# Decoding one of two weight matrices in natural order and exchanging its columns later, with a new instruction plan

## The chip, the cores and the metric

The kernel runs on 1 core of one Trainium2 chip. The metric is the device time of one execution in microseconds (us), as the median of several runs. In texts and rows below, PE is TensorE, which does the matrix products (PEld its loads of weights), DVE is VectorE, ACT is ScalarE, POOL is GpSimd and SP is SyncE, whose queue issues the transfers (DMAs).

## What is computed

Attention with pooled keys and values over 8 batches, 8 heads, 576 positions and 64 columns, and then a layer of 4608 tokens whose activation is a rational function. Cut to what matters:

```
k_p, v_p = k, v averaged over groups of 8 positions        # 72 keys per head
attn = softmax(q @ k_p^T / sqrt(64));  x = attn @ v_p       # x: 4608 x 512
h = x @ w_in                                               # w_in: 512 x 2048
P = a0 + a1 h + a2 h^2 + a3 h^3
Q = 1 + |b0| |h| + |b1| h^2
out = (P / (Q + 1e-6)) @ w_out                             # w_out: 2048 x 512
```

The two weight matrices arrive as 64-bit floating-point numbers, two 32-bit words each, and the kernel makes 32-bit numbers of them itself (the decoding).

## The kernel before

**Tiling.** The 4608 tokens are 18 blocks (i) of 256, the 2048 hidden columns 8 slices (u) of 256. A step is a pair (i, u). `mm1` multiplies x of the block by slice u of w_in into a bank of PSUM `ph`. It makes 24 products of 256 columns, since x and the weights are each split into a high part and a low part (`x0`, `x1`; `w[:, 0]`, `w[:, 1]`) and three of the four pairings are kept. `rational` and `quotient` turn `ph` into the activation on ACT, DVE and POOL, with the tiles `t`, `w`, `r`, `rp` (a PSUM bank) and the results `gh` (high, ACT) and `gl` (low, POOL). `mm2` multiplies these by slice u of w_out, 12 products of 512 columns, into two PSUM banks `po`, which collect over the slices. `po` leaves through `ob` to memory. All PSUM tiles share 8 banks.

**Attention** (`prep_k`, `prep_v`, `attention`, `values`) is computed block by block between these steps: q is transposed (`qT`, from block 4 on by DVE, before that by PE as `pq`), the scores go to `ps`, DVE takes maximum and difference into `e`, ACT the exponential, the transposed probabilities are `am`, and the product with the values is `pv`, which becomes `x0`, `x1`.

**Decoding** (`load_weights`, line 489) is done once for each of the 16 slices (8 of w_in, 8 of w_out), one at a time when a slice is first needed, in the first 200 us. A load of 1 MiB brings 128 x 1024 pairs of words (`rwin`, `rwout`). Then five instructions follow, each on 128 x 1024 elements: ACT scales the high words (Prelu) into `m`; DVE shifts `m`; DVE joins it with the low words (`scalar_tensor_tensor`); ACT copies `m` to the high part, rounding it; POOL subtracts this from `m` for the low part. The pool `dec` of the tile `m` has two buffers. For w_in, ACT and DVE read every second word (8 bytes apart) and write next to each other. For w_out, the columns change places as they are decoded: even and odd columns come to lie in two halves, as `mm2` reads them. So they read every fourth word (16 bytes apart), one half after the other, and copy and subtraction work on neighbouring elements:

```
words = raw.bitcast(I32).rearrange("p (n b t) -> p t b n", b=2, t=2)
hw, lw = words[:, 1], words[:, 0]
whole, bits = (y.rearrange("p (b n) -> p b n", b=2) for y in (m, mi))
```

**Order.** Every instruction is recorded by the class `Plan` with an engine, an assumed length and a due time, and `solve` puts them in an order: of what can start next on an engine, that with the earliest due time goes first. `issue` writes them out, so that all go through one line, L307 in the trace. The assumed lengths come from `Engine` (a fixed part and a rate per element); an argument such as `W + 260` lengthens one. Due times come from `due` (constants `HEAD`, `PACE`, `SLOW`, line 939), go back along the dependences, and are moved by the table `LATER` (line 114), which gives for an instruction's number the us by which it is due later. Where the plan has PE idle, `issue` puts in products that change nothing (fillers, L299): at first onto the tile `idle`, later with a zero operand onto an open `po`.

Of the kernel before, what the change touches and what calls it, by code (L numbers as in the profile page):

```python
# [8 lines left out]
F32 = mybir.dt.float32  # L9
F32R = mybir.dt.float32r  # L10
I32 = mybir.dt.int32
# [88 lines left out]
class Plan:  # L100
# [13 lines left out]
    LATER = {  # L114
# [12 lines left out]
    }  # L127
# [198 lines left out]
def tile_pooled_attention_then_rational_moe(  # L326
# [162 lines left out]
    def load_weights(kind, u):  # L489
        name = f"{kind}{u}"  # L490
        raw = new("cpool", name, [P, 2 * CW], F32, "r" + name)
        if kind == "win":
            dma(1024, raw.bitcast(I32).rearrange("p (k x) -> p k x", x=4 * P),
                w_in32[:, u * 4 * P:(u + 1) * 4 * P].rearrange("(k p) x -> p k x", p=P))
        else:
            dma(1024, raw.bitcast(I32).rearrange("p (f x) -> p f x", f=2),
                w_out32[u * 2 * P:(u + 1) * 2 * P, :].rearrange("(f p) x -> p f x", p=P), run=4096)
        m = new("dec", "m", [P, CW], F32, f"m_{name}")
        mi = m.bitcast(I32)
        if kind == "win":  # L500
            words = raw.bitcast(I32).rearrange("p (n t) -> p t n", t=2)
            hw, lw = words[:, 1], words[:, 0]
            whole, bits = m, mi
        else:

            words = raw.bitcast(I32).rearrange("p (n b t) -> p t b n", b=2, t=2)
            hw, lw = words[:, 1], words[:, 0]
            whole, bits = (y.rearrange("p (b n) -> p b n", b=2) for y in (m, mi))
        act(CW + 100).activation(whole, hw.bitcast(F32), AF.Prelu, scale=2.0 ** -111, alpha=-2.0 ** 32)
        dve(CW, port=True, rate=0.52).tensor_scalar(  # L510
            out=mi, in0=mi, scalar1=3, scalar2=None, op0=ALU.logical_shift_left)
        dve(CW, port=True).scalar_tensor_tensor(
            out=bits, in0=lw, scalar=29, in1=bits, op0=ALU.logical_shift_right,
            op1=ALU.bitwise_or)
        w = new("cpool", name, [P, 2, CW], F32R, name)
        act(CW).copy(w[:, 0, :], m)
        gp(CW).tensor_tensor(out=w[:, 1, :], in0=m, in1=w[:, 0, :].bitcast(F32),
                             op=ALU.subtract)
        weights[kind, u] = w
# [108 lines left out]
    def split_v(n, vs, vrs, port):  # L628
        vhi, vlo = vm[n % 2]
        for hh, msk in enumerate((mlo, mhi)):  # L630
            cols = slice(hh * D, (hh + 1) * D)
            act(NJ * D + 100).activation(vhi[:, :, cols], vs, AF.Copy, scale=msk)
            dve(NJ * D, port=port).scalar_tensor_tensor(
                out=vlo[:, :, cols], in0=vs, scalar=msk,
                in1=vhi[:, :, cols].bitcast(F32), op0=ALU.mult, op1=ALU.subtract)
        r = vr[n % 2].rearrange("p (c m) x -> p c m x", m=2)
        for m in range(2):
            dst = r[:, :, m, :]
            act(2 * D + 100).activation(dst, vrs, AF.Copy, scale=mrem_lo[m])
            dve(2 * D, port=port).scalar_tensor_tensor(  # L640
                out=dst, in0=vrs, scalar=mrem[m], in1=dst.bitcast(F32),
# [31 lines left out]
    def attention(t, hi, lo, qs, es):  # L673
# [34 lines left out]
        for c in range(2):  # L708
# [9 lines left out]
        ef = es[:, 0:NJ, t % 2]  # L718
        act(H * SP).activation(ef, ef, AF.Exp, scale=D ** -0.5)
        dve(H * SP).tensor_reduce(out=sm.rearrange("p (j h) -> p j h", h=2), in_=e, op=ALU.add,  # L720
                                  axis=AX.X)
        dve(0).tensor_scalar(out=sm, in0=sm, scalar1=1e-9, scalar2=None, op0=ALU.add)
        dve(40).reciprocal(sm, sm)
# [135 lines left out]
    def quotient(W, h, t, w, r, rp, gh, gl, early, late):  # L859
# [14 lines left out]
            out=t, in0=rp, scalar=-2.0, in1=t, op0=ALU.add, op1=ALU.mult)  # L874
        act(W, claims=late).copy(gh, t)
        gp(W).tensor_tensor(out=gl, in0=t, in1=gh.bitcast(F32), op=ALU.subtract)
# [61 lines left out]
    order += [(i, u) for i in range(4, NBLK) for u in range(NU)]  # L938
    HEAD, PACE, SLOW, SLOWS = 15.0, 5.4, 5.0, 2 * NA

# [80 lines left out]
```

## Time and profile before

| | us |
|---|---|
| median of 3 runs | 941.05 (940.32 to 942.04) |
| the profiled execution | 940.58 |
| its span, first to last instruction | 938.9 |
| PE busy | 897.4 (96%) |
| DVE busy | 775.9 (83%) |
| ACT busy | 697.5 (74%) |
| POOL busy | 529.1 (56%) |
| mean granted clock of PE | 0.994 of full speed |

The profiled execution lasted 1.7 us longer than its span and is 0.05% below the median. Busy time of PE contains the fillers and the time by which single products are late, so that it is read with the pace of the products beside it. Most transfers of inputs and weights are in the first 80 us, where the 16 DMA engines are near fully busy; later they are a third busy or less.

### The profile page before, as it was taken

The page shows a single profiled execution, that of the slowest core. Times are in us where ns is not written, and L with a number is a line of the kernel's source. Part 1 is how long each engine was busy: PE and PEld are TensorE (multiplying, and loading weights), DVE is VectorE, ACT ScalarE, POOL GpSimd, SP SyncE. Part 2 cuts the span into 40 slices and gives each one's busy share as a digit, 9 for nine tenths or more (in the row PEclk, how much of TensorE's full clock was granted, in tenths as well). Part 3 has the DMA queues.
Part 4 walks back from the last instruction along what each step waited for, and adds up shares of the span by engine and source line. Part 5 has one row for each costly group of instructions (what it writes and reads, how often), then busy time and mean ns, then how long its engine had stood idle before and what let it go on. Part 6 is the DMA issues. An engine that isn't in the chain of part 4 may idle for free.

```text
span 938.9 us, 17065 instructions
## 1 busy us (share of the span) xinstructions
PE 897.4 (96%) x6157; PEld 830.8 (88%) x6157; DVE 775.9 (83%) x1337; ACT 697.5 (74%) x1124; POOL 529.1 (56%) x472
## 2 busy tenths in 40 slices
PE   8888998899999999999999999999989999999997
PEld 7877987898898999898998889998989999999996
DVE  7799987788988888887989699969797888787674
ACT  4888887777766776867786767686857787777774
POOL 4776775667355645454754474456544654445443
PEclk9999999999999999999999999999999999999999
DMA  9993210146143503030522252123413321202000
GB/s 310 309 386 115 62 36 1 45 123 146 48 90 77 122 6 73 9 65 22 126 61 43 49 121 71 27 53 90 103 25 62 89 58 20 61 1 57 1 24 23
DMA packets 185081, 75.33 MB, mean 80 GB/s; under 512 B 162340, under 2 KB 162340, under 8 KB 184996
## 3 DMA queue, kind: packets, MB, share of 16 engines
q1 hardware_dynamic: 184996, 74.23, 31.1%
q8 instruction: 49, 0.80, 0.3%
q14 instruction: 36, 0.29, 0.1%
HBM read 50.59 MB, written 12.58 MB: 67 GB/s over the span
## 4 chain that ended last, share of the span: by engine, by line
DVE 28%; PE 28%; ACT 16%; issue 9%; POOL 9%; SPq 6%; DMA 3%; DVEq 0%; POOLq 0%; ACTq 0%
PE ph L307 13%; PE po L307 12%; DVE t L307 12%; SPq L307 6%; POOL w L307 5%; ACT rp L307 4%; DVE rp L307 3%; POOL gl L307 3%; DVE m_wout L307 2%; ACT gh L307 2%; DVE e L307 2%; PE ps L307 2%; ACT w L307 2%; ACT r L307 2%; ACT t L307 2%
## 5 line engine op out<-in xcount | busy, mean ns | idle before, releaser
L307 PEld LDWEIGHTS ph<-x,win 128*128 128x128 f32 x3264 | 461.6, 192 | 41.0 <-ACT x L307 3.5
L307 PE MATMUL ph<-x,win 128*128 128x256 f32 x3264 | 473.1, 277 | 6.9 <-ACT x L307 2.5
L307 PE MATMUL po<-wout,gh 128*128 128x512 f32 x1152 | 335.9, 386 | 10.5 <-ACT gh L307 8.1
L307 POOL TENSOR_TENSOR w<-w,r 128x512 f32<-128x512 f32 (+1 forms) x145 | 192.3, 1327 | 260.5 <-ACT r L307 252.2
L307 POOL TENSOR_TENSOR gl<-t,gh 128x512 fp32r<-128x512 f32 (+1 forms) x145 | 189.5, 1307 | 96.3 <-ACT gh L307 86.6
L307 PEld LDWEIGHTS po<-wout,gh 128*128 128x128 f32 x1152 | 186.9, 192 | 22.9 <-ACT gh L307 10.9
L307 PE MATMUL po<-wout,gl 128*128 128x512 f32 x576 | 171.8, 383 | 0.8 <-POOL gl L307 0.8
L307 DVE SCALAR_TENSOR_TENSOR t<-t,abn,rp 128x512 f32<-128x512 f32 (+1 forms) x145 | 107.0, 738 | 69.4 <-ACT rp L307 68.4
L307 ACT ACTIVATE rp<-w,cbias 128x512 f32<-128x512 f32 (+1 forms) x145 | 99.7, 688 | 53.6 <-POOL w L307 48.9
L307 ACT ACTIVATE w<-ph 128x512 f32<-128x512 f32 (+1 forms) x145 | 85.6, 591 | 60.8 <-DVE t L307 35.4
L307 DVE TENSOR_TENSOR t<-t,ph 128x512 f32<-128x512 f32 (+1 forms) x145 | 97.8, 674 | 38.3 <-ACT t L307 32.9
L307 ACT ACTIVATE t<-ph,abn 128x512 f32<-128x512 f32 (+1 forms) x145 | 111.6, 770 | 17.4 <-PE ph L307 10.4
L307 ACT ACTIVATE r<-w,abn 128x512 f32<-128x512 f32 (+1 forms) x145 | 117.4, 810 | 8.9 <-POOL gl L307 2.8
L307 ACT CAST gh<-t 128x512 fp32r<-128x512 f32 (+1 forms) x145 | 89.0, 614 | 40.7 <-DVE t L307 40.1
L307 DVE SCALAR_TENSOR_TENSOR t<-t,abn,ph 128x512 f32<-128x512 f32 (+1 forms) x145 | 106.5, 735 | 7.3 <-ACT w L307 3.8
L307 DVE SCALAR_TENSOR_TENSOR t<-rp,t 128x512 f32<-128x512 f32 (+1 forms) x145 | 98.4, 679 | 1.8
L307 DVE SCALAR_TENSOR_TENSOR rp<-w,rp 128x512 f32<-128x512 f32 (+1 forms) x145 | 98.9, 682 | 0.9 <-ACT rp L307 0.5
L307 PEld LDWEIGHTS po<-wout,gl 128*128 128x128 f32 x576 | 92.2, 191 | 5.6 <-POOL gl L307 2.0
L307 ACT ACTIVATE rp<-rp 128x512 f32<-128x512 f32 (+1 forms) x145 | 84.0, 579 | 2.9 <-DVE t L307 0.5
L307 POOL TENSOR_TENSOR e<-e,sm 128x576 f32<-128x576 f32 x36 | 41.6, 1170 | 29.3 <-DVE sm L307 23.0
L307 PE MATMUL ps<-kpT,qT 128*128 128x144 f32 (+1 forms) x304 | 45.4, 299 | 8.8 <-DVE qT L307 5.9
L307 PEld LDWEIGHTS ps<-kpT,qT 128*128 128x128 f32 (+1 forms) x304 | 37.3, 181 | 15.8 <-DVE qT L307 7.4
(109 smaller groups left out, 883.2 us busy)
## 6 DMA issues: line engine op xcount, KB each, us to landing
am<-e SPq DMA_DIRECT2D x224, 48.0 KB, 2.1
out_dram<-ob SPq DMA_DIRECT2D x17, 512.0 KB, 3.5
rwin<-in_moe_w_in_dram SPq DMA_DIRECT2D x8, 1024.0 KB, 12.2
rwout<-in_moe_w_out_dram SPq DMA_DIRECT2D x8, 1024.0 KB, 14.6
st_k<-in_k_dram SPq DMA_DIRECT2D x12, 512.0 KB, 4.6
st_v<-in_v_dram SPq DMA_DIRECT2D x12, 512.0 KB, 3.8
q<-in_q_dram SPq DMA_DIRECT2D x144, 32.0 KB, 2.0
st_v<-in_v_dram SPq DMA_DIRECT2D x48, 64.0 KB, 2.2
```

Of the source, the lines that this page charges most:

```text
L307: getattr(engines[op.eng], name)(*map(value, args), **{k: value(v) for k, v in kw.items()})
```

## The change

`load_weights` no longer treats w_out apart up to the joined `m`: ACT and DVE read every second word, and `m` is in natural order. The columns change places in the last two instructions: the copy (ACT) and the subtraction (POOL) read `m` at every second element (8 bytes apart) and write the two halves. `mm2` is as it was. The plan gets other assumed lengths (Prelu of the decoding, the low parts of the values, exp, the copy to `gh`), one small DVE instruction of the softmax is planned as one that needs the port which DVE and POOL share, steps are due 5.5 and then 5.8 us apart in place of 5.0 and 5.4, and `LATER` has other numbers (they reach to instruction 4701; before, to 1655).

```diff
     LATER = {
-        40: -21840.4, 45: -7931.8, 50: -6005.5, 61: -3867.9, 77: -7203.6, 85: -2.3, 99: -5839.5,
...
+        1: -25, 40: -21825, 45: -7954, 50: -6055, 61: -3895, 77: -7198, 85: 11, 99: -5792, 127: 63,
...
-        if kind == "win":
-            words = raw.bitcast(I32).rearrange("p (n t) -> p t n", t=2)
-            hw, lw = words[:, 1], words[:, 0]
-            whole, bits = m, mi
-        else:
-
-            words = raw.bitcast(I32).rearrange("p (n b t) -> p t b n", b=2, t=2)
-            hw, lw = words[:, 1], words[:, 0]
-            whole, bits = (y.rearrange("p (b n) -> p b n", b=2) for y in (m, mi))
-        act(CW + 100).activation(whole, hw.bitcast(F32), AF.Prelu, scale=2.0 ** -111, alpha=-2.0 ** 32)
+        words = raw.bitcast(I32).rearrange("p (n t) -> p t n", t=2)
+        hw, lw = words[:, 1], words[:, 0]
+        act(CW + 200).activation(m, hw.bitcast(F32), AF.Prelu, scale=2.0 ** -111, alpha=-2.0 ** 32)
...
         dve(CW, port=True).scalar_tensor_tensor(
-            out=bits, in0=lw, scalar=29, in1=bits, op0=ALU.logical_shift_right,
+            out=mi, in0=lw, scalar=29, in1=mi, op0=ALU.logical_shift_right,
             op1=ALU.bitwise_or)
         w = new("cpool", name, [P, 2, CW], F32R, name)
-        act(CW).copy(w[:, 0, :], m)
-        gp(CW).tensor_tensor(out=w[:, 1, :], in0=m, in1=w[:, 0, :].bitcast(F32),
-                             op=ALU.subtract)
+        high, low = w[:, 0, :], w[:, 1, :]
+        if kind == "wout":
+
+            m, high, low = (m.rearrange("p (n b) -> p b n", b=2),
+                            *(x.rearrange("p (b n) -> p b n", b=2) for x in (high, low)))
+        act(CW).copy(high, m)
+        gp(CW).tensor_tensor(out=low, in0=m, in1=high.bitcast(F32), op=ALU.subtract)
...
-            dve(NJ * D, port=port).scalar_tensor_tensor(
+            dve(NJ * D + 50, port=port).scalar_tensor_tensor(
...
-        act(H * SP).activation(ef, ef, AF.Exp, scale=D ** -0.5)
+        act(H * SP + 36).activation(ef, ef, AF.Exp, scale=D ** -0.5)
...
-        dve(0).tensor_scalar(out=sm, in0=sm, scalar1=1e-9, scalar2=None, op0=ALU.add)
+        dve(0, port=True).tensor_scalar(out=sm, in0=sm, scalar1=1e-9, scalar2=None, op0=ALU.add)
...
-        act(W, claims=late).copy(gh, t)
+        act(W + 26, claims=late).copy(gh, t)
...
-    HEAD, PACE, SLOW, SLOWS = 15.0, 5.4, 5.0, 2 * NA
+    HEAD, PACE, SLOW, SLOWS = 15.0, 5.8, 5.5, 2 * NA
```

No engine's instructions change in kind or number but for the fillers: 52 onto `idle` and 29 onto `po` before, 54 and 6 with the change. What stands in another order is seen at three places.

On DVE, while w_out's slices 5 and 6 are decoded (`m_wout5`, `m_wout6`; `t2_5`, `rp2_5` belong to the activation of block 2, slice 5; `abn` holds constants). Before:

```order
L307 SCALAR_TENSOR_TENSOR t2_6_1996<-t2_6_1996,abn_494,ph2_6_1883 128x512
L307 SCALAR_TENSOR_TENSOR m_wout5_1845<-rwout5_807,m_wout5_1845 128x1024
L307 SCALAR_TENSOR_TENSOR m_wout6_1969<-rwout6_744,m_wout6_1969 128x1024
L307 SCALAR_TENSOR_TENSOR t2_5_1984<-t2_5_1984,abn_494,rp2_5_2025 128x512
L307 SCALAR_TENSOR_TENSOR rp2_5_2025<-w2_5_1979,rp2_5_2025 128x512
```

With the change:

```order
L321 SCALAR_TENSOR_TENSOR t2_6_1979<-t2_6_1979,abn_503,ph2_6_1896 128x512
L321 SCALAR_TENSOR_TENSOR m_wout5_1894<-rwout5_831,m_wout5_1894 128x1024
L321 SCALAR_TENSOR_TENSOR t2_5_1913<-t2_5_1913,abn_503,rp2_5_2008 128x512
L321 SCALAR_TENSOR_TENSOR rp2_5_2008<-w2_5_1963,rp2_5_2008 128x512
L321 SCALAR_TENSOR_TENSOR t2_5_1913<-rp2_5_2008,t2_5_1913 128x512
L321 TENSOR_TENSOR t2_7_2041<-t2_7_2041,ph2_7_1954 128x512
L321 SCALAR_TENSOR_TENSOR t2_7_2041<-t2_7_2041,abn_503,ph2_7_1954 128x512
L321 TENSOR_SCALAR m_wout6_1989<-m_wout6_1989 128x1024
L321 TENSOR_SCALAR m_wout7_2070<-m_wout7_2070 128x1024
L321 SCALAR_TENSOR_TENSOR m_wout6_1989<-rwout6_822,m_wout6_1989 128x1024
```

The activation of slice 5 stood behind two joining instructions of the decoding and now stands behind one.

On PE, where the products with the values of block 13 (`pv13`) are done and the scores of the 28th and 29th half block of queries (`ps28`, `ps29`, which read DVE's `qT29`) come next. Before, the end of the stretch from the last `pv13` to `ps29`:

```order
L307 MATMUL ph12_7_8271<-x0_12_7717,win7_1805 128x256 x4
L307 MATMUL ps28_0_8371<-kpT0_99,qT28_7940 128x144 x2
L307 MATMUL ps28_1_8374<-kpT0_99,qT28_7940 128x144 x2
L307 MATMUL po12_0_0_8027<-wout4_1924,gl12_4_8287 128x512
L307 MATMUL po12_0_1_8029<-wout4_1924,gl12_4_8287 128x512
L307 MATMUL ph12_7_8271<-x1_12_7726,win7_1805 128x256 x4
L307 MATMUL ph13_0_8388<-x0_13_8335,win0_371 128x256 x4
L307 MATMUL ps29_0_8398<-kpT0_99,qT29_8380 128x144 x2
```

With the change, the end of the same stretch:

```order
L321 MATMUL ph13_0_8336<-x0_13_8269,win0_371 128x256 x8
L321 MATMUL ph13_0_8336<-x1_13_8277,win0_371 128x256 x4
L321 MATMUL ps28_0_8354<-kpT0_103,qT28_7917 128x144 x2
L321 MATMUL ps28_1_8359<-kpT0_103,qT28_7917 128x144 x2
L321 MATMUL ph13_0_8336<-x0_13_8269,win0_371 128x256 x8
L321 MATMUL ps29_1_8379<-kpT0_103,qT29_8369 128x144 x2
```

In the whole stretch stood 20 products for `ph` and 6 for `po`; now stand 40 and 6. On DVE, four instructions stood from behind the second `x1_13` to `qT29` (the transposition included); now it is six, all of the activation but one maximum and the transposition.

On SP's queue, the loads behind those of block 2's queries (`q2`). Before:

```order
L307 DMA q2_443<-in_q_dram 128x8x64
L307 DMA rwin3_462<-in_moe_w_in_dram 128x4x512
L307 DMA rwout3_470<-in_moe_w_out_dram 128x2x1024
L307 DMA early1_1_339<-in_v_dram 16x2x512
L307 DMA xd1_0_557<-x1_0_402 128x1024
```

With the change:

```order
L321 DMA q2_435<-in_q_dram 128x8x64
L321 DMA rwout3_451<-in_moe_w_out_dram 128x2x1024
L321 DMA rwin7_459<-in_moe_w_in_dram 128x4x512
L321 DMA rwin3_496<-in_moe_w_in_dram 128x4x512
L321 DMA early1_1_338<-in_v_dram 16x2x512
```

The load of w_in's slice 3 was the first of the three behind `q2` and is now the third, behind two of 1 MiB.

## Rows read from the trace of the kernel before

**Rows 1.** The page: span, and busy time of each engine.

```profile
span 938.9 us, 17065 instructions
PE 897.4 (96%) x6157; PEld 830.8 (88%) x6157; DVE 775.9 (83%) x1337; ACT 697.5 (74%) x1124; POOL 529.1 (56%) x472
```

**Rows 2.** Windows: stretch, then busy us of the five engines, granted clock, DMA.

```profile
20.00:200.00 180.00, 162.97 (x1132) 149.19 (x1132) 153.67 (x225) 149.65 (x228) 126.10 (x84) 0.98 0.43 140
200.00:920.00 720.00, 703.51 (x4858) 655.13 (x4857) 600.98 (x1065) 532.05 (x866) 386.21 (x329) 1.00 0.28 61
160.00:180.00 20.00, 17.23 (x99) 15.88 (x98) 17.08 (x19) 14.53 (x19) 14.23 (x8) 0.85 0.15 53
```

**Rows 3.** Waits of PE from 20 to 200 us: total us, times, longest.

```profile
PE po L307 <- ACT gh L307: 3.7, 2, 2.8
PE ph L307 <- DVE t L307: 2.3, 1, 2.3
PE po L307 <- ACT wout L307: 2.0, 2, 1.0
PE ph L307 <- ACT win L307: 1.4, 1, 1.4
```

**Rows 4.** Groups by form: xcount | busy us, mean ns | idle before, releasers.

```profile
L307 DVE SCALAR_TENSOR_TENSOR m_wout<-rwout,m_wout 128x1024 int32<-128x1024 int32 x8 | 22.3, 2801 | 0.1
L307 POOL TENSOR_TENSOR wout<-m_wout,wout 128x1024 fp32r<-128x1024 f32 x8 | 21.0, 2628 | 0.3
L307 ACT ACTIVATE m_wout<-rwout 128x1024 f32<-128x1024 f32 x8 | 19.2, 2406 | 1.8 <-POOL win L307 1.4 <-POOL wout L307 0.4
L307 DVE SCALAR_TENSOR_TENSOR m_win<-rwin,m_win 128x1024 int32<-128x1024 int32 x8 | 12.4, 1549 | 0.0
L307 ACT ACTIVATE m_win<-rwin 128x1024 f32<-128x1024 f32 x8 | 10.4, 1303 | 0.1
L307 ACT CAST wout<-m_wout 128x1024 fp32r<-128x1024 f32 x8 | 8.4, 1046 | 6.4 <-DVE m_wout L307 6.4
L299 PE MATMUL po<-zero,identr 128*128 128x256 f32 x29 | 4.5, 282 | 0.0
```

**Rows 5.** Timeline of PE, 152 to 180 us: start, us, instruction, [idle before].

```profile
152.33 3.29 PE L307 MATMUL ph<-x,win 128*128 128x256 f32 x28
...
159.70 4.55 PE L307 MATMUL ph<-x,win 128*128 128x256 f32 x24 [2.34 <-DVE t L307]
164.08 1.03 PE L307 MATMUL po<-wout,gh 128*128 128x512 f32 x4
...
177.96 2.08 PE L307 MATMUL po<-wout,gh 128*128 128x512 f32 x4 [2.77 <-ACT gh L307]
```

**Rows 6.** Timeline of ACT and DVE in the same part of the span.

```profile
138.20 2.87 ACT L307 ACTIVATE m_wout<-rwout 128x1024 f32<-128x1024 f32 x1
...
154.11 3.46 DVE L307 SCALAR_TENSOR_TENSOR m_wout<-rwout,m_wout 128x1024 int32<-128x1024 int32 x1
...
168.35 6.30 DVE L307 SCALAR_TENSOR_TENSOR m_wout<-rwout,m_wout 128x1024 int32<-128x1024 int32 x2
```

**Rows 7.** Waits of PE from 200 to 920 us: the two largest.

```profile
PE ps L307 <- DVE qT L307: 5.9, 5, 2.3
PE po L307 <- ACT gh L307: 4.4, 9, 0.7
```

**Rows 8.** Timeline of DVE and PE at the scores of `ps29`.

```profile
691.75 0.70 DVE L307 STREAM_TRANSPOSE qT<-q 128x512 f32<-128x512 f32 x1
...
692.51 1.05 PE L307 MATMUL ps<-kpT,qT 128*128 128x144 f32 x4 [2.27 <-DVE qT L307]
```

**Rows 9.** Timeline of SP and ACT; last, w_in's loads, from issue to landing.

```profile
41.94 0.47 SPq L307 DMA_DIRECT2D early<-in_v_dram  x1
...
53.77 1.57 ACT L307 ACTIVATE m_win<-rwin 128x1024 f32<-128x1024 f32 x1
...
DMA to landing us min/median/max: 8.4/12.2/15.6
```

More of the change, by code (lines that the diff above doesn't have):

```diff
@@ L639, in split_v @@
             act(2 * D + 100).activation(dst, vrs, AF.Copy, scale=mrem_lo[m])
-            dve(2 * D, port=port).scalar_tensor_tensor(
+            dve(2 * D + 50, port=port).scalar_tensor_tensor(
                 out=dst, in0=vrs, scalar=mrem[m], in1=dst.bitcast(F32),
```

36 rows, old and new, of the table LATER are left out of this document.

## The prediction

> **What bounds the kernel now.** I read the page's busy times first: PE is busy for 897.4 of 938.9 us and no other engine for more than 83% [rows 1]. So an instruction saved on ACT or DVE is worth only what it takes out of a wait of PE, and the question is where PE waits. The windows answer that: from 20 to 200 us PE is idle for 180 - 162.97 = 17.0 us, in the 720 us behind that for 16.5 us [rows 2]. The early part is thus four times as dense in waits, and it is the part in which the weights are decoded. There the granted clock also falls once, to 0.85 of full speed from 160 to 180 us [rows 2], that is, for some of that time to the lower of its two levels. The waits of PE by releaser come next [rows 3]: they name the activation's results on ACT and DVE and the decoded parts of the weights. Last I read what a decoding costs by form [rows 4]: joining takes DVE 2801 ns for w_out and 1549 ns for w_in, the Prelu ACT 2406 ns and 1303 ns, for the same number of elements. The only difference is the order in which the words are read: 16 bytes apart or 8.
>
> **The decoding, per slice of w_out.** The Prelu and the joining become those of w_in: ACT saves 2406 - 1303 = 1.10 us, DVE 2801 - 1549 = 1.25 us, over eight slices 8.8 and 10.0 us. The copy now reads 8 bytes apart; between nothing and the difference of w_in's Prelu to the copy (1303 - 1046 = 0.26 us) I take nothing, since it reads one stream and writes neighbours, as before. The subtraction on POOL (2628 ns) has no row with a stride. Below, it costs nothing more; above, it grows as ACT did between 8 and 16 bytes, by 2406/1303, that is by 2.2 us. I take nothing: its nearest row is its own, and the new stride is the one at which ACT and DVE do w_in. The shift on DVE stays as it is.
>
> [...]
>
> **What of this is on PE's path.** At 154.11 us a joining holds DVE for 3.46 us [rows 6]; behind it stands the activation that gives PE its next bank, and PE waits 2.34 us [rows 5]. With 1.55 in place of 3.46 us, 1.9 us of that wait go. After it, PE makes 24 products in 4.55 us; at the pace of the row before (28 in 3.29 us, 0.1175 us each) they take 2.82 us [rows 5]. This is the stretch with the clock of 0.85, and 1.7 us go if the wait does. At 168.35 us two joinings in a row hold DVE for 6.30 us [rows 6] and PE waits 2.77 us for the `gh` behind them [rows 5]. At 3.1 us the whole wait goes, the more so since the new order has the activation between the two. The four products behind it take 2.08 instead of 1.03 us [rows 5], so another 1.05. The other early wait for `gh` is 3.7 - 2.8 = 0.9 us [rows 3]; a Prelu of 2.87 us on ACT stands ahead [rows 6], which loses 1.57, so it goes. Together 1.9 + 1.7 + 2.8 + 1.0 + 0.9 = **8.3 us**.
>
> PE waits twice, 2.0 us in all, directly for a decoded slice of w_out [rows 3]. Each such chain is 2.35 us shorter: **2.0 us** go. These releases cost nothing elsewhere as long as PE has other work; what is late next is a subtraction on POOL.
>
> **The order.** The plan has 29 fillers on open sums [rows 4] and with the change 6. A filler is real time on PE, 4.5 us for 29, 0.155 each, so 23 fewer are 3.6 us; but they fill waits that may come back as idle time. Between 0 and 3.6 I take **1.8 us**, the middle, having no row that is nearer to one end.
>
> On SP's queue, w_in's slice 3 changes from first to third behind q's load. The third was issued at 41.94 us; from issue to landing these loads take 8.4 to 15.6 us, 12.2 in the middle [rows 9]. So it lands at 50.3 to 57.5 us, likely 54.1, where ACT began on it at 53.77 us [rows 9]. What is queued behind that Prelu on ACT is the activation, and PE waits 1.4 us for this slice already [rows 3]. The cost is between 0 and 3.7 us; by the median, **0.4 us** is lost.
>
> From 200 us on nothing is decoded, and only order and due times differ. The largest waits there are `ps` for DVE's transposed queries, 5.9 us, and `po` for `gh`, 4.4 us [rows 7]. The longest, 2.27 us before 692.51, ends with a transposition of 0.70 us [rows 8]. There the new order gives PE 20 more products ahead of the waiting scores (20 x 0.1175 = 2.35 us), and DVE two more instructions ahead of the transposition's end (2 x 0.70 = 1.4 us), so that some 0.95 of 2.27 us are gained, four tenths. I take a third of the 10.3 us as the gain of this part, **3.4 us**, since this is one place of many; the ends are a loss as large and a gain of two thirds of all 16.5 us, 11 us.
>
> The assumed lengths themselves issue nothing, and the instruction marked for the shared port is the same instruction: their cost is in the order alone.
>
> **Sum.** 8.3 + 2.0 + 1.8 + 3.4 - 0.4 = 15.1 us less. From the profiled execution's 940.6 us that gives 925.5 us; the median of the runs is 0.5 us above it, so I predict **926 us**.
>
> **The rivals.**
> - *POOL takes over* (slower). If the strided subtraction costs as much as the upper bound, a slice's chain is as long as before, only that POOL ends it, and the point from which it decides is an excess of 2.1 to 2.35 us, what the chain saves. Behind each subtraction on POOL stand products and low parts of the activation. ACT and DVE had 8 x 2.35 = 18.8 us of excess and PE paid 10.3 us for it, 55%; 8 x 2.2 = 17.6 us on POOL would cost 9.7 us, with the decoding's gain gone and nothing won in the order: 950 us. For it: no row shows such a read, and POOL is busy for 126 of these 180 us [rows 2]. Against: ACT and DVE show no such cost at 8 bytes.
> - *The cover holds* (no change). PE is 96% busy, and the waits that go come back behind it for other reasons; only the direct 2.0 us are won, and slice 3's load takes 0.4: 939.5 us. Against: the two longest waits have the joining itself in front.
> - *The later part loses.* The new order from 200 us on adds a third to the waits instead of taking it: 925.5 + 6.8 = 932 us. Nothing in the trace excludes it.
> - *The plan keeps step.* With lengths nearer to the trace, two thirds of the 16.5 us go, and all 3.6 us of fillers: 925.5 - 7.6 - 1.8 = 916 us.
> - *The stride was not what cost.* If the 1.1 and 1.25 us come from something else about w_out, the change doesn't do what it says, the decoding stays as long and only the order counts: 940.6 - 1.8 - 3.4 + 0.4 = 936 us. [...] The rows leave little room for it, as nothing else differs between the two forms.
>
> **How the numbers follow.** I give the forecast (920 to 932 us) 0.57, the plan that keeps step 0.15, the later part that loses 0.10, the stride that did not cost 0.03, the cover 0.07 and POOL 0.08. A measurement of this kernel tells a difference of about 0.2%, 1.9 us, from none. Faster by more than that hold the first four, 0.85; within it the cover, 0.07; slower POOL, 0.08. The range from 914 to 940 us takes in the bounds of fillers, load and later part, and leaves out POOL and a little at each end.
>
> **What would show it.** Right: joining and Prelu of w_out at about 1.55 and 1.3 us, copy near 1.05 and subtraction near 2.6 us; no wait of PE over 1 us between 140 and 180 us, and a granted clock of 1.00 there; idle time of PE from 20 to 200 us of 8 to 11 us instead of 17.0, and from 200 to 920 us of 10 to 14 instead of 16.5. Wrong: a subtraction above 4 us with waits of PE on `gl` or `wout` from POOL; a wait of several us on w_in's slice 3 near 70 us; or the same idle time as before from 200 us on.

## The result, and the profile after

The change takes **912.24 us** (median of 4 runs, 911.21 to 913.83) against 940.68 us of the kernel before (4 runs beside them, 940.26 to 942.04): a ratio of 0.9697 [0.9679, 0.9714], 28.4 us less. The forecast was 926 us; the direction was right, the gain nearly twice as large, and the time lies 1.8 us below the range.

The page of the changed kernel has these busy times (its profiled execution took 911.21 us):

```profile
span 909.5 us, 17035 instructions
PE 887.0 (98%) x6136; PEld 821.8 (90%) x6136; DVE 770.0 (85%) x1337; ACT 691.5 (76%) x1124; POOL 522.2 (57%) x472
```

Against [rows 1] PE is busy for 10.4 us less and idle for 22.5 instead of 41.5 us. So a third of what was won is busy time of PE: it has 23 fillers less on `po` (29 before, 6 now), and less of its work falls at the lower granted clock (0.50 of full speed from 161 to 163 us in the trace of before), as the next rows show. The windows of the changed kernel (columns as in [rows 2]):

```profile
20.00:200.00 180.00, 173.34 (x1222) 158.10 (x1221) 158.30 (x256) 152.25 (x244) 132.05 (x95) 1.00 0.48 149
160.00:180.00 20.00, 19.80 (x132) 17.72 (x130) 17.15 (x21) 15.61 (x22) 15.30 (x10) 1.00 0.11 35
200.00:900.00 700.00, 691.67 (x4785) 643.82 (x4786) 595.45 (x1047) 529.95 (x864) 378.42 (x323) 1.00 0.27 60
```

From 20 to 200 us PE is now idle for 6.7 instead of 17.0 us, and where the clock was 0.85 it is 1.00. From 140 to 180 us PE has one wait left:

```profile
155.97 0.70 PE L321 MATMUL po<-wout,gh 128*128 128x512 f32 x2 [1.00 <-ACT gh L321]
```

From 200 to 900 us it is idle for 8.3 us. The decoding of w_out, by form:

```profile
L321 POOL TENSOR_TENSOR wout<-m_wout,wout 128x1024 fp32r<-128x1024 f32 x8 | 19.5, 2435 | 5.4 <-ACT wout L321 5.2 <-PE po L321 0.2
L321 DVE SCALAR_TENSOR_TENSOR m_wout<-rwout,m_wout 128x1024 int32<-128x1024 int32 x8 | 11.8, 1483 | 0.0
L321 ACT ACTIVATE m_wout<-rwout 128x1024 f32<-128x1024 f32 x8 | 11.2, 1396 | 0.8 <-POOL win L321 0.7 <-POOL wout L321 0.2
L321 ACT CAST wout<-m_wout 128x1024 fp32r<-128x1024 f32 x8 | 10.9, 1363 | 2.7 <-DVE m_wout L321 2.7
```

Against [rows 4], joining and Prelu became what the same reading takes for w_in. The copy became longer (1046 to 1363 ns), and the subtraction on POOL no longer but a little shorter (2628 to 2435 ns).

**Where the time was won.** Windows at the same time hold different work in the two kernels. At the first and at the last write of a finished block PE has done nearly the same work (1142 and 1137 products without fillers at the first), so I read these on SP's queue (start, us, instruction). Writes in the middle serve less well, since orders differ in which block they bring forward. Before:

```profile
197.78 0.68 SPq L307 DMA_DIRECT2D out_dram<-ob  x1
...
900.76 35.15 SPq L307 DMA_DIRECT2D out_dram<-ob  x3
```

After:

```profile
180.83 0.67 SPq L321 DMA_DIRECT2D out_dram<-ob  x1
...
904.82 1.75 SPq L321 DMA_DIRECT2D out_dram<-ob  x2
```

To the first write 17.0 us are won (197.8 to 180.8), from there to the end of the last one another 12.3 (900.76 + 35.15 - 197.78 = 738.1 us, and 904.82 + 1.75 - 180.83 = 725.7 us). How the second part is made up shows in windows over this stretch. Before, with the one 20 us window from 200 to 920 us whose clock is below 1.00:

```profile
680.00:700.00 20.00, 17.60 (x122) 16.41 (x121) 18.84 (x37) 12.07 (x20) 8.54 (x7) 0.91 0.13 25
...
198.00:935.00 737.00, 719.50 (x4937) 667.78 (x4936) 610.85 (x1082) 541.52 (x886) 394.23 (x337) 1.00 0.27 60
```

After:

```profile
181.00:906.00 725.00, 715.48 (x4938) 665.22 (x4936) 615.00 (x1085) 544.97 (x890) 393.57 (x338) 1.00 0.28 61
```

With nearly the same number of products, idle time falls from 17.5 to 9.5 us and busy time by 4.0 us. Of the 4.0 us I estimate some 1.8 to be the clock from 680 to 700 us (20 x 0.09; the 2.27 us wait of [rows 8] lies there), and no window of after has a clock below 1.00 in this part. Five fillers of 0.15 us are another 0.7 us; where the rest was I could not place. The waits of PE from 200 to 900 us, after (columns as in [rows 3]):

```profile
PE po L321 <- ACT gh L321: 5.0, 9, 1.1
PE pv L321 <- DVE am L321: 1.5, 2, 0.8
PE ph L321 <- DVE t L321: 0.7, 1, 0.7
PE ps L321 <- DVE kpT L321: 0.3, 1, 0.3
```

The largest row of before, 5.9 us of `ps` for `qT` [rows 7], is gone; the wait for `gh` is little changed.

### The profile page after: what moved, and what is told of

Same layout as the page of the kernel before. It is cut to its first block, busy times and chain, and to the rows that moved or that the text cites. A ratio compares the mean times of both kernels' runs of the same rounds, so it can differ in the third digit from the quotient of the medians.

```text
span 909.5 us, 17035 instructions
## 1 busy us (share of the span) xinstructions
PE 887.0 (98%) x6136; PEld 821.8 (90%) x6136; DVE 770.0 (85%) x1337; ACT 691.5 (76%) x1124; POOL 522.2 (57%) x472
## 4 chain that ended last, share of the span: by engine, by line
PE 37%; DVE 17%; ACT 12%; POOL 9%; issue 8%; SPq 5%; DMA 3%; DVEq 0%; POOLq 0%; ACTq 0%
PE ph L321 17%; PE po L321 16%; DVE t L321 8%; SPq L321 5%; POOL w L321 3%; ACT rp L321 3%; POOL gl L321 3%; ACT t L321 2%; DVE rp L321 2%; PE ps L321 2%; PE pv L321 2%; ACT gh L321 1%; ACT w L321 1%; DMA q<-in_q_dram 1%; DMA st_v<-in_v_dram 1%
## 5 line engine op out<-in xcount | busy, mean ns | idle before, releaser
L321 PEld LDWEIGHTS ph<-x,win 128*128 128x128 f32 x3264 | 423.8, 191 | 24.7 <-issue 1.7
L321 PE MATMUL ph<-x,win 128*128 128x256 f32 x3264 | 435.0, 276 | 1.5 <-DVE t L321 0.7
L321 PE MATMUL po<-wout,gh 128*128 128x512 f32 x1152 | 320.8, 383 | 6.8 <-ACT gh L321 6.0
L321 POOL TENSOR_TENSOR w<-w,r 128x512 f32<-128x512 f32 (+1 forms) x145 | 187.8, 1295 | 219.4 <-ACT r L321 204.2
L321 PEld LDWEIGHTS po<-wout,gh 128*128 128x128 f32 x1152 | 196.9, 190 | 27.7 <-ACT gh L321 9.9
L321 PE MATMUL po<-wout,gl 128*128 128x512 f32 x576 | 173.8, 383 | 0.1
L321 ACT ACTIVATE t<-ph,abn 128x512 f32<-128x512 f32 (+1 forms) x145 | 111.9, 773 | 30.5 <-DVE rp L321 12.3
L321 PEld LDWEIGHTS po<-wout,gl 128*128 128x128 f32 x576 | 97.8, 190 | 9.1 <-POOL gl L321 1.5
L321 PE MATMUL pv<-am,vm 128*128 128x256 f32 (+3 forms) x288 | 47.0, 279 | 1.1 <-DVE am L321 0.8
L321 PEld LDWEIGHTS pv<-am,vm 128*128 128x128 f32 x288 | 42.3, 190 | 2.6 <-DVE am L321 1.4
## 6 DMA issues: line engine op xcount, KB each, us to landing
rwin<-in_moe_w_in_dram SPq DMA_DIRECT2D x8, 1024.0 KB, 13.2
rwout<-in_moe_w_out_dram SPq DMA_DIRECT2D x8, 1024.0 KB, 13.3
```

The costliest lines, as they stand in the source:

```text
L321: getattr(engines[op.eng], name)(*map(value, args), **{k: value(v) for k, v in kw.items()})
```

## The experiments

The kernel before ran beside each group and took 940.3 to 941.2 us, so that medians of different groups are compared within some 0.9 us. The runs of one kernel lie 1.3 to 5.5 us apart, so that a difference of about 2 us between two medians is barely told from none.

### e1: the new decoding in the old order

The kernel before, with the lines of the change in `load_weights` but the old assumed length, so that every engine keeps the order of before:

```diff
-        act(CW + 100).activation(whole, hw.bitcast(F32), AF.Prelu, scale=2.0 ** -111, alpha=-2.0 ** 32)
+        act(CW + 100).activation(m, hw.bitcast(F32), AF.Prelu, scale=2.0 ** -111, alpha=-2.0 ** 32)
...
+            m, high, low = (m.rearrange("p (n b) -> p b n", b=2),
+                            *(x.rearrange("p (b n) -> p b n", b=2) for x in (high, low)))
+        act(CW).copy(high, m)
```

> The order of before on every engine, with only the new decoding (Prelu and joining read 8 bytes apart, columns exchanged by copy and subtraction). Theory D (the prediction's own: the shorter decoding takes 10.3 us out of PE's waits in the first 200 us, whatever the order): 930 us, granted clock 1.00 from 160 to 180 us, PE idle 6 to 8 us less from 20 to 200 us. Theory O (what counts is an order made for the lengths that the decoding really has; in the old order the time saved is lost in the next wait): 936 us or more.

**925.39 us**, 0.9838 [0.9816, 0.9861]: 15.0 us, more than the 10.3 of the forecast's two decoding terms. The first write starts at 182.6 us, 15.2 earlier than before, and the rest is as before. Windows of before:

```profile
40.00:100.00 60.00, 53.67 (x389) 48.60 (x389) 56.52 (x84) 51.81 (x85) 41.73 (x29) 1.00 0.67 235
140.00:180.00 40.00, 33.13 (x200) 30.11 (x199) 31.49 (x36) 31.12 (x40) 25.58 (x14) 0.93 0.08 27
```

and of this kernel:

```profile
40.00:100.00 60.00, 59.31 (x430) 54.07 (x429) 55.67 (x94) 54.32 (x90) 44.10 (x34) 1.00 0.67 233
140.00:180.00 40.00, 38.54 (x260) 35.37 (x259) 34.02 (x46) 34.41 (x48) 29.75 (x19) 1.00 0.09 32
```

From 140 to 180 us idle time falls from 6.9 to 1.5 us and the clock rises from 0.93 to 1.00, as forecast. The surplus is from 40 to 100 us, where the first four slices of w_out are decoded: idle time falls from 6.3 to 0.7 us. Beside the two waits of 1.0 us for a slice of w_out, the longest of before in this part are:

```profile
71.59 0.71 PE L307 MATMUL ph<-x,win 128*128 128x256 f32 x4 [1.42 <-ACT win L307]
77.17 0.73 PE L307 MATMUL ps<-kpT,qT 128*128 128x144 f32 x4 [0.88 <-DVE sm L307]
90.17 0.41 PE L307 MATMUL pr<-identr,e 128*128 128x128 f32 x2 [1.33 <-DVE am L307]
```

All three are gone in e1, where PE's only wait from 40 to 100 us is one of 0.32 us for `wout`. Its waits from 200 to 900 us are those of before [rows 7], nearly to the number:

```profile
PE ps L307 <- DVE qT L307: 5.9, 5, 2.3
PE po L307 <- ACT gh L307: 4.0, 9, 0.7
```

### e2: the new order with the old decoding

The changed kernel with the old body of `load_weights` and the new assumed length, so that every engine has the order of after:

```diff
-        act(CW + 200).activation(m, hw.bitcast(F32), AF.Prelu, scale=2.0 ** -111, alpha=-2.0 ** 32)
+        act(CW + 200).activation(whole, hw.bitcast(F32), AF.Prelu, scale=2.0 ** -111, alpha=-2.0 ** 32)
...
-        act(CW).copy(high, m)
+        act(CW).copy(w[:, 0, :], m)
```

> The order of the change on every engine, with the old decoding. Theory D: the decoding's 10.3 us come back on top of the change's 912.2: 922 us. Theory O: order alone holds most of the gain, 914 to 917 us. A third, that the two need each other (the new order has less room around each decoding): 926 us or more, with PE waiting over 2 us behind a joining between 120 and 180 us.

**922.42 us**, 0.9801 [0.9781, 0.9821]: 18.0 us. The order alone is worth more than the decoding alone. Together they give 28.4 and not 15.0 + 18.0 = 33.0: the decoding brings 922.4 - 912.2 = 10.2 us in the new order, the order 925.4 - 912.2 = 13.2 us with the new decoding. Its writes on SP's queue:

```profile
190.57 0.67 SPq L321 DMA_DIRECT2D out_dram<-ob  x1
...
915.08 1.75 SPq L321 DMA_DIRECT2D out_dram<-ob  x2
```

Between the first and the end of the last lie 726.3 us, as in the changed kernel (725.7). So the later gain is the order's, and has nothing to do with the decoding. Before the first write, order alone brings 7.2 us of the 17.0 and the decoding alone 15.2 (e1): some 5.4 us either of them would bring.

### e5, e6: Prelu alone and joining alone

In the kernel before only one of the two instructions on w_out reads every second word. The high words and the low words are then in different orders, so that words of different columns are joined.

```diff
-            whole, bits = (y.rearrange("p (b n) -> p b n", b=2) for y in (m, mi))
+            whole, bits = m, mi.rearrange("p (b n) -> p b n", b=2)
-        act(CW + 100).activation(whole, hw.bitcast(F32), AF.Prelu, scale=2.0 ** -111, alpha=-2.0 ** 32)
+        act(CW + 100).activation(whole, raw.bitcast(I32).rearrange("p (n t) -> p t n", t=2)[:, 1].bitcast(F32), AF.Prelu, scale=2.0 ** -111, alpha=-2.0 ** 32)
```

> The kernel before, with only ACT's Prelu of w_out reading 8 bytes apart in natural order; the joining stays at 16 bytes, so high and low words of different columns are joined. The decoding alone (e1_decode_only) gave 15.0 us. If PE waited on the joining (DVE), as the prediction put the two longest waits: 3 to 5 us less than before, 936 us. If ACT's part weighs by its length (1.0 of 2.2 us saved in a chain): 7 us less, 933.5 us. If either half alone frees the chain: 12 us less, 928 us.

```diff
-            whole, bits = (y.rearrange("p (b n) -> p b n", b=2) for y in (m, mi))
+            whole, bits = m.rearrange("p (b n) -> p b n", b=2), mi
+            lw = raw.bitcast(I32).rearrange("p (n t) -> p t n", t=2)[:, 0]
```

> The kernel before, with only DVE's joining of w_out reading 8 bytes apart in natural order; the Prelu stays at 16 bytes, so high and low words of different columns are joined. If PE waited on the joining: 10 to 12 us less than before, 929 us, with the waits of 2.3 and 2.8 us between 150 and 180 us gone. If it weighs by its length: 8 us, 932.5 us. If the Prelu was the one: 4 us, 936 us.

Prelu alone: **933.13 us**, 0.9915 [0.989, 0.994], 7.2 us. Joining alone: **934.23 us**, 0.9923 [0.9899, 0.9947], 6.1 us. Together 13.3 of the 15.0 us. The Prelu is worth no less than the joining: 7.2 us is what it was expected to bring if it counts by its length, and the joining stays below the 8 us of that case. The timeline of PE shows which wait belongs to which. Prelu alone:

```profile
154.17 2.92 PE L307 MATMUL ph<-x,win 128*128 128x256 f32 x24 [1.23 <-DVE t L307]
...
170.84 2.08 PE L307 MATMUL po<-wout,gh 128*128 128x512 f32 x4 [2.82 <-ACT gh L307]
```

Joining alone:

```profile
157.46 2.92 PE L307 MATMUL ph<-x,win 128*128 128x256 f32 x24 [1.29 <-DVE t L307]
...
163.74 1.99 PE L307 MATMUL po<-wout,gh 128*128 128x512 f32 x8 [0.77 <-ACT gh L307]
```

The wait of 2.77 us for `gh` [rows 5] stays with the shorter Prelu and goes with the shorter joining (one of 0.77 us is left at 163.74 us): it is the one behind two joinings. The early wait of 0.96 us for `gh` goes with the shorter Prelu and stays, at 0.99 us, with the shorter joining. The wait of 2.34 us is halved by either, and in these executions the slow stretch behind it goes too: 24 products take 2.92 us behind a wait of 1.2 us, and took 4.55 us behind one of 2.34 us [rows 5].

### e7, e8: assumed lengths alone, spacing alone

On e1, all the new assumed lengths and the mark for the port that DVE and POOL share (its old spacing and `LATER` kept; in the trace of before one instruction of the marked kind takes 0.15 us at 101.40 us and one 1.26 us at 304.12 us, where `gl` has POOL busy from 304.07 to 305.35 us):

```diff
-        act(H * SP).activation(ef, ef, AF.Exp, scale=D ** -0.5)
+        act(H * SP + 36).activation(ef, ef, AF.Exp, scale=D ** -0.5)
...
-        act(W, claims=late).copy(gh, t)
+        act(W + 26, claims=late).copy(gh, t)
```

> The order of before with the new decoding (925.4 us) and only the new assumed lengths and the marked port; table and spacing of the due times as before. e4_old_table, which has the new spacing too, gave 920.5. If the lengths remove the waits for the transposed queries from 200 us on (5.9 us): 919 to 921 us and under 2 us of that wait. If the spacing does: 925 us and the 5.9 us stay.

On e1, only the due times:

```diff
-    HEAD, PACE, SLOW, SLOWS = 15.0, 5.4, 5.0, 2 * NA
+    HEAD, PACE, SLOW, SLOWS = 15.0, 5.8, 5.5, 2 * NA
```

> The order of before with the new decoding (925.4 us) and only the due times 5.5 and 5.8 us apart; table and assumed lengths as before. If the lengths remove the waits for the transposed queries: 925 us and 5.9 us of that wait from 200 us on. If the spacing does: 919 to 921 us and under 2 us of it.

**924.42 us**, 0.9823 [0.9801, 0.9845], and **922.15 us**, 0.9797 [0.9773, 0.9822]: 1.0 and 3.2 us of the order's 13.2, the first not clear of the spread of the runs. With the new lengths `ps` still waits 5.8 us for `qT`, so alone they do not remove that wait. With the new spacing it falls to 3.1 us (to 1.1 us with both, in e4), while `ph` waits 3.9 us for ACT and `pv` 3.1 us for `am`, waits that e1 has at 1.4 us each.

### e4, e3: the new plan with the old table, and without the later entries

The changed kernel with the old `LATER`:

```diff
     LATER = {
-        1: -25, 40: -21825, 45: -7954, 50: -6055, 61: -3895, 77: -7198, 85: 11, 99: -5792, 127: 63,
+        40: -21840.4, 45: -7931.8, 50: -6005.5, 61: -3867.9, 77: -7203.6, 85: -2.3, 99: -5839.5,
...
```

> The change (new decoding, assumed lengths, marked port, due times 5.5 and 5.8 us apart) with the table of before. If the entries of the table carry what the decoding doesn't: 930 us, as the decoding alone, or worse, since the old table was made for other lengths. If lengths and spacing carry it: 912 to 918 us.

and with the new one up to number 1655, where the old one ends (137 entries less):

```diff
+        1653: -1.5, 1655: 5,
-        1663: 16, 1667: -10, 1730: 20, 1736: -3, 1785: 3, 1787: 10, 1868: 8, 1882: 11, 1890: 1,
...
-        4675: -5, 4701: 4,
```

> The change without the 137 entries of the table beyond instruction 1655, which leaves the order as the change has it up to about 270 us. If those entries carry the gain of the later part (12.8 us between the points of equal work at 200 us and at the end, where the prediction had 3.4): 924 to 926 us. If lengths and spacing of due times carry it: 912 to 915 us. The prediction's own third of the waits: 915.6 us.

With the old table **920.46 us**, 0.9778 [0.9753, 0.9802]: lengths and spacing together bring 4.9 us over e1, the table the other 8.2. Without the late entries **924.92 us**, 0.9826 [0.9802, 0.9851]: beside the new early ones these carry 12.7 us, nearly all that the order is worth. The waits of PE from 200 to 900 us without them:

```profile
PE pv L306 <- DVE am L306: 5.6, 4, 2.3
PE ph L306 <- ACT x L306: 2.8, 6, 0.7
PE ps L306 <- DVE qT L306: 1.4, 3, 0.6
```

So most of the wait for `qT` goes without them and one for `am` stands in its place, which the late entries take away.

That does not make the late entries the source of the gain. The writes of e4 (L307) and then of e3 (L306):

```profile
187.14 0.68 SPq L307 DMA_DIRECT2D out_dram<-ob  x1
...
912.73 1.75 SPq L307 DMA_DIRECT2D out_dram<-ob  x2
...
181.73 0.68 SPq L306 DMA_DIRECT2D out_dram<-ob  x1
...
915.50 1.75 SPq L306 DMA_DIRECT2D out_dram<-ob  x2
```

From the first write to the end of the last e4 takes 727.3 us, e3 735.5; e1 took 737.4 and the change takes 725.7. So lengths and spacing with the old table, which has no late entry, bring 10.0 of the 11.6 us of this part, and most of e4's loss is before the first write (187.1 against 180.8 us). With the early entries of the new table the same lengths and spacing bring 1.9 us, and the late entries are needed for the rest. Nor does e3 lose its time where entries are first missing. Windows (columns as in [rows 2]) of the change, then of e3, whose order on PE parts from that of the change at 272 us:

```profile
270.00:490.00 220.00, 217.25 (x1513) 202.84 (x1512) 196.64 (x351) 166.49 (x270) 119.60 (x103) 1.00 0.28 62
490.00:900.00 410.00, 406.47 (x2816) 378.00 (x2815) 338.80 (x592) 311.25 (x508) 219.74 (x187) 1.00 0.24 53
...
270.00:490.00 220.00, 216.92 (x1519) 203.12 (x1518) 194.70 (x346) 166.78 (x272) 121.63 (x104) 1.00 0.28 61
490.00:900.00 410.00, 400.23 (x2767) 374.54 (x2766) 332.78 (x584) 304.29 (x493) 211.72 (x181) 0.99 0.24 54
```

Up to 490 us it keeps up; behind that it makes 49 products fewer.

### e12, e11: half of the late entries, and one of them

The changed kernel without the 79 entries above 3000, by which PE keeps the order of the change up to some 470 us, and without the entry 1663 alone:

```diff
-        2877: 3, 2896: 9, 2997: -26, 3000: 4, 3003: 6, 3015: -6, 3028: 3.01, 3038: -15, 3052: -2,
+        2877: 3, 2896: 9, 2997: -26, 3000: 4,
...
```

> The change without the 79 entries of the table beyond instruction 3000; PE's order is the change's for its first 3025 of 5943 products, up to about 450 us. Without any entry beyond 1655 it was 924.9 us (12.7 more). If each stretch's entries carry that stretch's gain: equal progress with the change up to 450 us, then a loss of some 7 us spread over the rest, 918 to 920 us. If the entries up to 3000 bring the kernel into a state that then keeps: 912 to 914 us. If entries work only as a whole: 922 us or more.

```diff
-        1663: 16, 1667: -10, 1730: 20, 1736: -3, 1785: 3, 1787: 10, 1868: 8, 1882: 11, 1890: 1,
+        1667: -10, 1730: 20, 1736: -3, 1785: 3, 1787: 10, 1868: 8, 1882: 11, 1890: 1,
```

> The change without one entry of the table (instruction 1663, 16 us later); the order of PE is the same for the first 1789 products, up to about 280 us. If the gain of the later part comes from something that any order with these lengths and entries has: 911 to 914 us. If it belongs to this one order, which the table was fitted to: 916 us or more, with waits for pv or for transposed queries back.

Without half: **919.27 us**, 0.9759 [0.9743, 0.9775], 7.0 us of the 12.7. Its profiled execution took 923.28 us, the longest of its five, and the places below are read from that one. The write of a block in the middle of the order stands at 451.58 us against 449.07 in the changed kernel, and the first one at 182.30 against 180.83: of 2.5 us, 1.5 were there at the start, and the rest of the 12.1 us by which this execution is longer is lost behind it. 4.0 us of that are this execution's own, by which it is above the median of its kernel: its mean clock is 0.990, that of three others 0.998. Its waits of PE from 450 to 915 us:

```profile
PE pv L312 <- DVE am L312: 2.6, 2, 1.7
PE ph L312 <- ACT x L312: 2.2, 4, 0.8
PE ps L312 <- DVE qT L312: 1.4, 3, 0.8
```

The longest of these in the timeline:

```profile
762.06 0.30 PE L312 MATMUL pv<-am,vr 128*64 128x192 f32 x1 [1.74 <-DVE am L312]
```

and the window it lies in:

```profile
760.00:780.00 20.00, 18.26 (x113) 17.18 (x112) 16.66 (x32) 12.97 (x21) 5.82 (x6) 0.83 0.11 18
```

In the changed kernel the largest in this part is `gh` with 2.4 us, the next 0.7. Here the wait of 1.74 us costs more than itself: the clock of these 20 us is 0.83, and two products for `po` take 1.20 us at 767.11 us, where two before the wait took 0.60. It need not: e4 also waits 1.74 us for `am`, at 760.65 us, and its clock from 760 to 780 us is 1.00.

Without one entry: **914.41 us**, 0.9723 [0.9709, 0.9738], 2.2 us slower than the change, between the two expectations; a wait for `qT` of 1.6 us and one for `am` of 1.9 us come back. Its order parts from that of the change at 287 us. From 290 to 440 us it makes 1039 products on PE and the change 1029; from 440 to 540 us 685 and 706. So this loss, too, comes far behind the entry, and that each stretch's entries carry that stretch's gain is not shown.

### e9: one wait taken away by itself

On e1, the scores of every second half block from the 11th on are planned 2.0 us behind their inputs:

```diff
-            pe(1350 if len(sg) > 1 else 244 * 2, part, claims=(e, mx, sm))
+            given = pe(1350 if len(sg) > 1 else 244 * 2, part, claims=(e, mx, sm))
+            given.lead = 2.0 if t > 10 and t % 2 else 0.0
```

> The order of before with the new decoding (925.4 us) and one more rule of the plan: from the 11th half block on, the scores of every second half block are planned 2.0 us after their inputs, so that PE has some six products for po and four for ph more ahead of the transposed queries. If the waits for transposed queries (5.9 us from 200 us on, and the slow clock behind the longest) are a loss of their own: under 2 us of them and 918 to 920 us. If other waits take their place: under 2 us of them and 924 to 926 us.

**923.18 us**, 0.9829 [0.9803, 0.9854]: 2.2 us less than e1 by the medians, with intervals that nearly coincide. The 5.9 us of `ps` for `qT` are gone, but these now lead:

```profile
PE po L307 <- ACT gh L307: 5.5, 11, 0.8
PE pv L307 <- DVE t L307: 1.8, 3, 1.5
PE pv L307 <- DVE am L307: 1.5, 2, 0.8
```

The first was 4.0 us in e1, the second was not among its waits. PE gets by one wait earlier to the next.

### e10: the exchange on the writing side

The changed kernel, but copy and subtraction go through `m` in its own order, read neighbours, and write by turns into the two halves:

```diff
-            m, high, low = (m.rearrange("p (n b) -> p b n", b=2),
-                            *(x.rearrange("p (b n) -> p b n", b=2) for x in (high, low)))
+            m, high, low = (m.rearrange("p (n b) -> p n b", b=2),
+                            *(x.rearrange("p (b n) -> p n b", b=2) for x in (high, low)))
```

> The change, but copy and subtraction of w_out go through m in natural order, so that they read neighbours and write in turn into the two halves. If the copy's 1363 ns (1046 before) come from reading 8 bytes apart: 1046 to 1100 ns. If writing in turn costs as much or more: 1363 ns or more. Theory D (a decoding's length still counts at 55%): 0.3 us in 8 copies give 1.4 us, 910.8 us. If the new order has room for it: 912 us, same.

**917.96 us**, 0.9765 [0.9748, 0.9781], 5.7 us slower than the change:

```profile
L321 POOL TENSOR_TENSOR wout<-m_wout,wout 128x1024 fp32r<-128x1024 f32 x8 | 21.5, 2688 | 9.2 <-ACT wout L321 9.1
L321 ACT CAST wout<-m_wout 128x1024 fp32r<-128x1024 f32 x8 | 16.4, 2053 | 2.1 <-DVE m_wout L321 2.1
```

The copy takes 0.69 us more than in the changed kernel, the subtraction 0.25, over eight slices 7.5 us, and the end comes 5.7 us later, three quarters of it. It is lost before the first write (187.56 against 180.83 us); behind it both take the same (725.9 and 725.7 us). The decoding is still paid for on PE's path in the new order.

## Why the prediction was right and wrong

**The mechanism of the decoding was right.** Joining and Prelu fell to 1483 and 1396 ns (forecast some 1.55 and 1.3 us), and POOL did not pay for it. So two rivals fall: POOL takes over, and the stride was not what cost. Read 8 and no longer 16 bytes apart, the words take DVE 1483 ns in place of 2801 and ACT 1396 ns in place of 2406. POOL's subtraction, which reads 8 bytes apart with the change, took 2435 ns against 2628 before.

**The place from 140 to 180 us was right**, 8.3 us forecast. In the changed kernel one wait is left there, 1.00 us for `gh`, and the clock is 1.00; e1 shows 5.4 us of idle time less plus the clock. e5 and e6 bear out which instruction stood ahead of which wait. They do not bear out the shares: the forecast gave the Prelu 0.9 of the 8.3 us and a part of the 2.0, and alone it is worth 7.2 us. It also halves the wait of 2.34 us, which the forecast put on the joining.

**The term "2.0 us, the direct waits for w_out" failed in size.** It counted only the waits that the profile puts down to a slice of w_out. From 40 to 100 us alone 5.6 us of idle time went with the decoding alone. There ACT and DVE were 86% and 94% busy in the windows of before, and what they made for other products came late as well: waits of 1.42 us for w_in, 1.33 for `am` and 0.88 for `sm` went with it. With 15.0 in place of 10.3 us the decoding in the old order was mis-sized by 4.7 us. That it is worth 10.2 us in the new order, almost the forecast's 10.3, is luck: the terms were read from waits of the old order.

**Fillers and the load, 1.8 - 0.4 = 1.4 us, about held.** With the decoding of e1 the first write stands at 182.58 us, with the new order at 180.83: 1.75 us. This is all that the new order does up to there; that the fillers did it is not shown. The load of w_in's slice 3 cost nothing: its Prelu begins at 54.19 us instead of 53.77, and PE waits for no slice of w_in. (It waits 1.08 us at 37.18 us for a load of v, which e1 does not.)

**The term "order from 200 us on, 3.4 us" failed most.** It came out at 12.3 us between first and last write, above even its upper end of 11 us; the likeliest rival, the plan that keeps step (916 us), came nearest. Two things were wrong in it. It was read at one place, `qT`, and a third of two waits was taken from there. But that wait by itself is worth hardly more than the 2.2 us of e9, while lengths and spacing together, which change many waits, bring 10.0 us behind the first write (e4). And its upper end was set by idle time alone. Idle time fell by 8.0 us, within that end; another 4.0 us of the 12 in the windows are PE's busy time, by the estimate above 1.8 of them the clock behind a wait. The rival came near in size, and its ground held only in part: less than half of the idle time went, not two thirds, and the new lengths alone bring 1.0 us (e7).

This term alone does not take the time below the range: 8.9 us more would give 917 us. The other terms make 8.3 + 2.0 + 1.8 - 0.4 = 11.7 us, and up to the first write 17.0 were won, 5.3 more, of which the decoding has 4.9 (15.2 in e1 for 10.3). Only both together give 912 us. The signs named for idle time of PE were passed as well: 6.7 us from 20 to 200 us (8 to 11 were named) and 8.3 us from 200 to 900 us (10 to 14, up to 920 us).

**The copy** was taken at nothing with 0.26 us as the bound; it grew by 0.32 us a slice, above the bound, which the measured gain of the decoding already contains.

**The rivals "the cover holds" and "the later part loses" fall**: the waits did not come back in the new order. They do come back when only one of them is taken away (e9).

**What stays open**: by which of its moves the new order wins the time behind the first write. It is the order's and not the decoding's (e2). Lengths and spacing get most of it with the old table (e4) and little with the early part of the new one (e3), so what a part of the plan carries depends on the other parts. None of the twelve is faster than the change.

## What to carry to other kernels

Compare two orders by landmarks of equal work, such as the first and the last write of a finished block, before reading any share: they say in which part the time went, and idle time and busy time between them say as what. Here, with the main engine 96% busy and many small waits, one wait removed was mostly paid again at the next (in e9 5.9 us of waiting went and 2.2 us were won); so bound an order that was shifted in many places by all of the idle time of the stretch and the slower products behind its waits, not by one place. Taking one part of a plan out says what it is worth beside the others, and another combination can say otherwise, as e3 and e4 do. And where a decoding holds two engines near their limit (here 86% and 94% busy), count more than the waits that bear its name: here it took 15.0 us (e1), where the waits that were read gave 10.3.

## What was not expected of the hardware

- **Copy of 128 x 1024 fp32 on ACT**: 1046 ns between neighbours, 1363 ns when it reads 8 bytes apart, 2053 ns when it reads neighbours and writes by turns into two halves. Here writing apart cost ACT more than reading apart. For POOL's subtraction it is 2628, 2435 and 2688 ns (in the last it also reads one operand by turns); between neighbours alone it takes 2388 to 2633 ns in e2, e5 and e6, so that no pattern is told from another.
- **The clock behind a wait of PE** did not go by the length of the wait alone. Behind 1.23 and 1.29 us 24 products took 2.92 us (2.84 us with no wait ahead of them, at 162.53 us of e5), and behind one of 2.34 us they took 4.55 us. But at the same place of the same order, behind the same wait, four products of the scores take 1.33 us in e1 and 0.76 us in e5, where the clock from 680 to 700 us is 1.00:

```profile
677.19 1.33 PE L307 MATMUL ps<-kpT,qT 128*128 128x144 f32 x4 [2.26 <-DVE qT L307]
...
687.06 0.76 PE L307 MATMUL ps<-kpT,qT 128*128 128x144 f32 x4 [2.26 <-DVE qT L307]
```

So what a wait of about 2 us cost beside itself differed between these two executions.
